# Weights times V as float32 products, both heads in turn on the two halves of TensorE's columns

## The chip, the core and the metric

The kernel runs on one core of a Trainium2 chip. In the profile its engines are PE (TensorE, the matmuls; PEld is its weight loads), DVE (VectorE), ACT (ScalarE), POOL (GpSimd) and SP (SyncE, which issues nearly all DMAs). The metric is the device time of one launch in microseconds, lower is better. Three runs of the kernel before gave 1402.59, 1403.88 and 1408.41 us.

## The reference

Attention with a band below the top score, and a gated feed-forward layer behind it, all in float32:

```
q, k, v: 8 batches x 8 heads x 576 x 64;  tau = 0.02
s    = q @ k.T / sqrt(64)                       per batch and head
keep = s >= max(s, row) - tau
a    = exp(s - max(s, row)) where keep, else 0
a    = a / (sum(a, row) + 1e-9)
x    = a @ v                                     -> 4608 tokens x 512
out  = (sigmoid(x @ w_gate) * (x @ w_val)) @ w_out   512 -> 1536 -> 512
```

## The kernel before, in words

A 576-token sequence is 4 tiles of 128 queries and 64 leftover queries. The attention works in visits, one for each batch (8) and pair of heads (4): 32 visits of 9 tiles: for each of the two heads (`h`) four query tiles, in groups of two, and one tile that holds the leftover queries of both heads (`h` is `None`, names with `_l`). The groups come in the order (`Visit.groups`): head 0 tiles 0 and 1, the leftover tile, head 0 tiles 2 and 3, head 1 tiles 0 and 1, head 1 tiles 2 and 3.

Most matmuls take their float32 operands as two float32r numbers each, a rounded high part and the remainder (low), and add three (or two) products; the first four visits (batch 0, `NPS` and `NPV`) do theirs as plain float32 matmuls, which stand in the profile as two records each. For a tile: the scores `s` (line 618, PE), the row maximum `st` (line 625, DVE), the threshold (line 630, ACT, or line 634, POOL), the exponential `p` (line 639, ACT), mask and row sum in one step (line 642, DVE). Then for a group: an addition to the sums (line 668, ACT, or 671, POOL), the reciprocal (line 674, DVE), and the scaling of `p` by POOL (line 687). PE transposes `p` into `tp` (line 702) and the leftover keys into `lk` (line 740, or 731 in the first four visits). In visits 4 to 31 the transposed weights are split: ACT copies the high part to `pt` (line 712), DVE subtracts for the low part (line 719), and the same for `pl` (lines 746 and 749); for a head's second group POOL copies the leftover queries' columns to the end of `pt` and `pl` (lines 759 and 762). V is loaded to `vn` and split into `vs` by ACT and POOL (lines 518 and 520). The product `av` (line 803) is nine matmuls a group and head, with V's high and low part side by side on the 128 columns of the stationary side; so the result's two halves of partitions are added, by a copy on ACT (line 806) and an addition on DVE (line 807), into `xf`. In the first four visits (line 790) the stationary side is V alone, 64 columns, so that one half of TensorE's columns is used; one copy on ACT (line 795) puts the result into `xf`.

The feed-forward layer works on blocks of 512 tokens. Blocks 0 to 4 go through `in_units` (`m`, line 861) and `out_units` (`o`, line 899), while attention runs on. The gate tile `th` is ACT's and then DVE's (lines 873 and 877). The last four blocks are taken two at a time (`two_blocks`) by Strassen's scheme: seven products p1 to p7 of sums of operands in place of eight (`qa`, `qb`, `qc`, line 1092; `ra`, `rb`, `rc`, line 1146); `token_sums` makes the operands (copies on ACT line 999, low parts on DVE line 1001, sums on POOL line 1006) and `chains` adds the results out of PSUM on DVE (lines 1029 and 1031). The weights come packed and are converted first, 36 tiles of them (`convert`: lines 425 to 469, with three steps on DVE, lines 441, 445 and 451, and two on POOL, lines 428 and 469).

The order of all instructions is written out before the program runs: `Plan.run` simulates the engines with the costs that each `op` carries, takes on each engine the ready operation with the smallest key for which buffers are free, and emits in that order. Keys count attention tiles: `LEAD` is how far ahead of its first tile a visit's loads are asked for, `SHIFT` a break in the keys ahead of batch 1, `CONV_IN` and `CONV_OUT` the first key and the step of the conversions, `SUMS` where the sums of weights for Strassen's scheme are spread. Feed-forward matmuls have keys above all attention, so they fill what attention leaves of PE. `SLOTS` is the number of buffers by tag; buffers of most tags are given in turn.

## Time and profile before

| | |
|---|---|
| median of three runs | 1403.88 us |
| the profiled execution: its time, its span | 1396.95 us, 1395.2 us |
| granted TensorE clock, mean | 0.999 |
| busy: PE, PEld | 1357.9, 1154.2 us |
| busy: DVE, ACT, POOL | 1097.0, 875.3, 801.4 us |
| DMA | 341.28 MB, mean 245 GB/s |
| first `m` to be gated on DVE (`th`) | 133.95 us |

In a row of groups stand: line, engine, operation, output<-inputs, shapes (partitions x elements), count; then busy time, mean ns of one; then the engine's idle time before them and what ended it. In a row of stretches: from:to, the length, and for each engine busy us and number of instructions, then the granted clock, the busy share of the DMA engines and GB/s. A row of waits names who waited, for whom, us in total, how often, and the longest. A row of the timeline begins with start and length in us. Matmuls overlap one another, so the distance from a start to the next one's start says more of PE than a length does.

### The profile page before, as it was taken

What the parts mean: (1) busy time and instruction counts of PE and PEld (TensorE: products, weight loads), DVE (VectorE), ACT (ScalarE), POOL (GpSimd) and SP (SyncE); (2) the same over time, 40 slices, a digit from 0 to 9 for tenths busy, and PEclk for the clock granted to TensorE, in tenths of its full rate; (3) what the DMA queues carried; (4) which work ended last, traced back from release to release, by engine and by line L of the source; (5) the groups of instructions that cost most, each with busy time, mean ns of one, the idle gap of its engine ahead of it and who ended that gap; (6) DMA issues with size and microseconds to landing.
All of it is one profiled execution on the core that took longest, in us unless ns stands there. A gap on an engine that the chain in (4) does not pass through costs nothing.

```text
span 1395.2 us, 23257 instructions
## 1 busy us (share of the span) xinstructions
PE 1357.9 (97%) x7472; PEld 1154.2 (83%) x7472; DVE 1097.0 (79%) x2144; ACT 875.3 (63%) x1930; POOL 801.4 (57%) x868
## 2 busy tenths in 40 slices
PE   7998999999999999999999999999999999899998
PEld 5666788888888888888888888888888887788886
DVE  7997989888788888888888888888936559645595
ACT  6877777677777777777777777777732235322242
POOL 5888765448787777786777976455420137001160
PEclk9999999999999999999999999999999999999999
DMA  7889888869999998899988999776567666665574
GB/s 266 279 248 314 303 260 238 230 205 264 267 261 330 292 278 250 261 289 296 304 267 242 303 295 277 200 224 198 160 223 227 201 195 202 202 199 187 184 225 137
DMA packets 142328, 341.28 MB, mean 245 GB/s; under 512 B 22784, under 2 KB 42752, under 8 KB 142208
## 3 DMA queue, kind: packets, MB, share of 16 engines
q1 hardware_dynamic: 142064, 339.80, 79.8%
q8 instruction: 61, 1.00, 0.3%
q14 instruction: 59, 0.48, 0.1%
q10 hardware_dynamic: 144, 0.00, 0.0%
HBM read 232.78 MB, written 55.57 MB: 207 GB/s over the span
## 4 chain that ended last, share of the span: by engine, by line
PE 78%; DMA 6%; DVE 6%; POOL 3%; ACT 2%; issue 2%; SPq 1%; DVEq 0%; ACTq 0%; POOLq 0%
PE m L861 17%; PE o L899 11%; PE s L618 9%; PE av L803 8%; PE qb L1092 7%; PE tp L702 6%; PE qa L1092 4%; PE qc L1092 4%; DMA su<-wid 4%; PE rb L1146 3%; PE av L790 2%; PE ra L1146 2%; PE rc L1146 2%; PE s_l L618 2%; POOL su L947 1%
## 5 line engine op out<-in xcount | busy, mean ns | idle before, releaser
L861 PE MATMUL m<-x,wi 128*128 128x512 f32 x1152 | 314.0, 403 | 0.0
L687 POOL TENSOR_SCALAR p<-p,w_t,sm 128x576 f32<-128x576 f32 x256 | 216.8, 857 | 91.5 <-DVE sm L674 80.7
L861 PEld LDWEIGHTS m<-x,wi 128*128 128x128 f32 x1152 | 200.9, 189 | 30.9
L642 DVE SCALAR_TENSOR_TENSOR p<-s,st,p 128x576 f32<-128x576 f32 x256 | 206.2, 812 | 23.0 <-ACT p L639 18.6
L625 DVE TENSOR_REDUCE st<-s 128x1 f32<-128x576 f32 x256 | 190.4, 751 | 34.1 <-PE s L618 30.1
L899 PE MATMUL o<-g,wo 128*128 128x512 f32 x720 | 194.3, 403 | 0.0
L639 ACT ACTIVATE p<-s,st 128x576 f32<-128x576 f32 x256 | 188.8, 738 | 6.9 <-DVE st L625 5.4
L712 ACT CAST pt<-tp 128x512 fp32r<-128x512 f32 x224 | 128.2, 587 | 63.5 <-PE tp L702 59.4
L719 DVE TENSOR_TENSOR pt<-tp,pt 128x512 fp32r<-128x512 f32 x224 | 150.5, 684 | 18.3 <-ACT pt L712 16.3
L618 PE MATMUL s<-kd,qd 128*128 128x288 f32 x896 | 159.7, 301 | 4.9 <-DVE p L642 2.7
L618 PEld LDWEIGHTS s<-kd,qd 128*128 128x128 f32 x896 | 136.8, 188 | 23.0 <-issue 3.0
L702 PE MATMUL tp<-ident,p 128*128 128x128 f32 x1024 | 146.8, 273 | 1.9 <-ACT pl_l L737 1.4
L899 PEld LDWEIGHTS o<-g,wo 128*128 128x128 f32 x720 | 126.1, 189 | 20.6 <-PE tp_l L702 0.2
L803 PE MATMUL av<-pt,vs 128*128 128x320 f32 (+1 forms) x896 | 137.0, 295 | 1.7 <-DVE pt L719 1.7
L702 PEld LDWEIGHTS tp<-ident,p 128*128 128x128 f32 x1024 | 122.3, 140 | 19.1 <-issue 3.2
L803 PEld LDWEIGHTS av<-pt,vs 128*128 128x128 f32 x896 | 129.2, 188 | 9.1 <-POOL p L687 2.1
L1006 POOL TENSOR_TENSOR gA<-gA 128x512 f32<-128x512 f32 x12 | 16.2, 1347 | 206.4 <-DVE gA L1071 206.4
L883 POOL TENSOR_TENSOR g<-th,g 128x512 fp32r<-128x512 f32 x60 | 78.8, 1313 | 23.0 <-ACT g L881 21.4
L806 ACT COPY avt<-av 64x256 f32<-64x256 f32 x112 | 44.2, 394 | 58.2 <-PE av L803 56.4
L1029 DVE TENSOR_TENSOR qu<-qb,qp 128x512 f32<-128x512 f32 x48 | 33.2, 691 | 55.9 <-PE qb L1092 48.4
L807 DVE TENSOR_TENSOR xf<-av,avt 64x256 f32<-64x256 f32 x112 | 50.8, 453 | 32.3 <-ACT avt L806 31.1
L749 DVE TENSOR_TENSOR pl<-lk,pl 64x128 fp32r<-64x128 f32 x224 | 64.7, 289 | 13.8 <-ACT pl L746 7.3
(171 smaller groups left out, 2743.1 us busy)
## 6 DMA issues: line engine op xcount, KB each, us to landing
wi<-wid SPq DMA_DIRECT2D x96, 512.0 KB, 7.1
kd<-k SPq DMA_DIRECT2D x112, 320.0 KB, 8.1
wo<-wod SPq DMA_DIRECT2D x60, 512.0 KB, 7.6
qd<-q SPq DMA_DIRECT2D x112, 128.0 KB, 6.1
wid<-ws SPq DMA_DIRECT2D x24, 512.0 KB, 4.5
su<-wid SPq DMA_DIRECT2D x24, 512.0 KB, 7.9
sid<-su SPq DMA_DIRECT2D x24, 512.0 KB, 4.6
wa<-wid SPq DMA_DIRECT2D x24, 512.0 KB, 4.5
```

The costliest lines, as they stand in the source:

```text
L618: nc.tensor.matmul(s.ap[:, c, :HALF], st(), mv(slice(k0 + c * HALF, k0 + (c + 1) * HALF)), start=m == 0, stop=m == len(steps) - 1,)
L625: op("DVE", 0.76, key, lambda: nc.vector.tensor_reduce(out=st.ap[:, 0:1], in_=sv(), axis=AX.XY, op=ALU.max, negate=True), reads=[s], write ...
L639: op("ACT", 0.74, key, lambda: nc.scalar.activation(p(), sv(), AF.Exp, bias=st.ap[:, 0:1], scale=1.0), reads=[s, (st, 0)], writes=[(g.p, i)])
L642: op("DVE", 0.9, key, lambda: nc.vector.scalar_tensor_tensor(out=p(), in0=sv(), scalar=st.ap[:, 1:2], in1=p(), op0=ALU.is_ge, op1=ALU.mult ...
L687: op("POOL", 0.9, key, lambda i=i: nc.gpsimd.tensor_scalar(out=p.ap[:, i * S : (i + 1) * S], in0=p.ap[:, i * S : (i + 1) * S], scalar1=w_t ...
L702: nc.tensor.matmul(tp.ap[:, c, :], self.p.ap[:, o + c * P : o + (c + 1) * P], ident, is_transpose=True, start=c == 0, stop=c == NJ - 1, sk ...
L712: op("ACT", 0.58, key, lambda: nc.scalar.copy(hi(), tp.ap), reads=[tp], writes=[(self.pt, (0, i))])
L719: op("DVE", 0.69, key, lambda: nc.vector.tensor_tensor(out=lo(), in0=tp.ap, in1=f32(hi()), op=ALU.subtract), reads=[tp, (self.pt, (0, i))] ...
L803: nc.tensor.matmul(av.ap, st, mv, start=i == 0, stop=i == len(ms) - 1)
L861: nc.tensor.matmul(m.ap, wv[:, a, c * P : (c + 1) * P], xs[c].ap[:, z, c0:c1], start=e == 0, stop=e == 11,)
L899: nc.tensor.matmul(acc.ap, wv[:, f, a], g[fg * ND + f].ap[:, z], start=(fg, f, a, z) == (0, 0, 0, 0), stop=(fg, f, a, z) == (NFG - 1, ND - ...
L1092: nc.tensor.matmul(acc.ap, wv[:, y, (2 * h + c) * P : (2 * h + c + 1) * P], xt[prod][c].get()[:, z], start=e == 0 and prod in FIRST, stop= ...
```

## The change

The split of the transposed weights and of V goes, in all visits. V is loaded as it is, with six column groups per head in place of five: the leftover keys' rows come twice, once with zeros in the second half of the partitions and once with zeros in the first half, so that the transposed leftover keys of two tiles (one `lk` of 128x128) can be used with all 128 rows. `pt` and `pl` hold both heads of a pair of tiles (`of_tiles`), and the product of both heads is one operation, issued after head 1's group: for each chunk of keys one float32 matmul of head 0 with its output on partitions 0 to 63 and one of head 1 on partitions 64 to 127, in turn. The leftover queries are multiplied from the leftover tile's own `pt` by matmuls of 64 columns. One copy by ACT puts both heads' result into `xf`. The addition to the sums goes; a factor on q that is zero where tau is negative, and a maximum on tau, take its place. POOL's scaling stays a tensor_scalar with two operations, whose first now adds a tile of zeros.

With it go: one more `t2` buffer and two tags moved in `chains`; other constants for the plan (`LEAD`, `CONV_IN`, `SHIFT`, `SUMS`); three of the output weights' conversions end on DVE instead of POOL (`DVE_LO_OUT`); `token_sums` puts some of POOL's subtractions on DVE (`X_BY`, `G_BY`) and one of them earlier; and `out_two` does, for every product but p1, all matmuls of one half of the outputs (`e`) ahead of the other's.

```diff
-    "w": 7, "t2": 5,
+    "w": 7, "t2": 6,
-LEAD = 8
-CONV_IN, CONV_OUT = (8, 2.2), (24, 3)
+LEAD = 3
+CONV_IN, CONV_OUT = (12, 2.2), (24, 3)
-NPS, NPV = 4, 4
+NPS = 4
+AV_COST = 0.0093
-SHIFT = 30
+SHIFT = 20
-DVE_LO_IN, DVE_LO_OUT = (), ()
+DVE_LO_IN, DVE_LO_OUT = (), range(6, 12, 2)
-SUMS = (36, 4)
+SUMS = (36, 6)
+X_BY = ((("POOL",) * 4, ("DVE",)), (("DVE",) * 4, ("DVE",)))
+G_BY = (("POOL", "DVE", "POOL", "DVE"), ("DVE",))
...
+            self.vs = buf("vs", [P, NJ + 2, 2, D], F32, f"vs{n}")
+            op("SP", 1.2, key - 3, lambda: nc.sync.dma_start(out=self.vs.ap, in_=v[b, hp]), writes=[self.vs])
...
         def normalise(self, key):
             sm, p, n = self.sm, self.p, self.n
-            if DEN(self.vis.first) == "ACT":
-                op("ACT", 0.3, key, lambda: nc.scalar.activation(sm.ap[:, :n], sm.ap[:, :n], AF.Identity, bias=den_t[:, 0:1]),
-                   writes=[sm])
...
             op("PE", 0.44, key, go, reads=[(self.p, i)], writes=[tp], also=[self.pt])
-            op("ACT", 0.58, key, lambda: nc.scalar.copy(hi(), tp.ap), reads=[tp], writes=[(self.pt, (0, i))])
...
-                op("DVE", 0.69, key, lambda: nc.vector.tensor_tensor(
-                    out=lo(), in0=tp.ap, in1=f32(hi()), op=ALU.subtract
-                ), reads=[tp, (self.pt, (0, i))], writes=[(self.pt, (1, i))])
+            op("ACT", 0.58, key, lambda: nc.scalar.copy(self.pt.ap[:, self.z, :, i * P : (i + 1) * P], tp.ap),
+               reads=[tp], writes=[(self.pt, (self.z, i))])
...
+        def output(self, c, key):
+            vis, pt, pl = self.vis, self.pt, self.pl
+            last = self.tiles[0] != 0
+            W = 2 * P + (SL if last else 0)
+            av = buf("b", [P, W], F32, f"av{self.name}", "att")
+            c0 = self.tiles[0] * P
+            ms = [(0, 2 * P, j, lambda h, j=j: pt.ap[:, h, j]) for j in range(NJ)]
+            ms += [(i * P, (i + 1) * P, NJ + i, lambda h: pl.ap[:, h]) for i in range(2)]
+            if last:
+                sl = lambda h: slice(h * SL, (h + 1) * SL)
+                ms += [(2 * P, W, j, lambda h, j=j: c.pt.ap[:, 0, j, sl(h)]) for j in range(NJ)]
+                ms += [(2 * P, W, NJ + 1, lambda h: c.pl.ap[:, 0, sl(h)])]
+            def go():
+                for i, (a, z, j, m) in enumerate(ms):
+                    for h in range(2):
                         nc.tensor.matmul(
+                            av.ap[h * D : (h + 1) * D, a:z], vis.vs.ap[:, j, h], m(h),
+                            start=i == 0, stop=i == len(ms) - 1, skip_group_check=True,
                         )
+            op("PE", AV_COST * W, key, go,
+               reads=[pt, pl] + ([c.pt, c.pl] if last else []) + [vis.vs], writes=[av], also=[vis.xf])
+            last_att[0] = op("ACT", act(W), key, lambda: nc.scalar.copy(vis.xf.ap[:, c0 : c0 + W], av.ap),
+                             reads=[av], writes=[(vis.xf, self.name)])
...
-                for e in range(2):
+                ws.append(w)
+            for g, e in [(g, e) for g in range(NFG) for e in range(2)] if prod == "p1" else [(g, e) for e in range(2) for g in range(NFG)]:
```

The plan's order moves in three places. The first is PE in visit 4 (batch 1, names `_0_`), while block 0's `m` runs: `av` is a product, `pt` and `pl` its transposed weights, `vs` V. Before, head 0's first pair of tiles:

```order
L861 MATMUL m_3_0_0_1807<-x_0_593,ws_0_619 128x512 x2
L803 MATMUL av_0_00_1816<-pt_0_00_1686,vs_0_1193 128x256 x8
L803 MATMUL av_0_00_1816<-pl_0_00_1754,vs_0_1193 128x256
L861 MATMUL m_3_0_0_1807<-x_0_593,ws_0_619 128x512
L861 MATMUL m_3_0_0_1807<-x_1_909,ws_0_619 128x512
```

and in the change, both heads' first pair, ahead of it the last transpose of leftover keys that it needs (`lk`):

```order
L673 MATMUL lk_0_10_1824<-ident,p_0_10_1661 128x128
L757 MATMUL m_4_1_0_1799<-x_2_1143,ws_1_970 128x512
L757 MATMUL m_4_1_0_1799<-x_3_1388,ws_1_970 128x512 x3
L757 MATMUL m_5_0_0_1834<-x_0_565,ws_0_1494 128x512 x3
L757 MATMUL m_5_0_0_1834<-x_1_848,ws_0_1494 128x512 x3
L595 MATMUL s_1_001_1849<-kd_1_0_1446,qd_1_0_1465 128x288 x4
L697 MATMUL av_0_10_1855<-pt_0_00_1614,vs_0_1135 64x256 x8
L697 MATMUL av_0_10_1855<-pl_0_00_1632,vs_0_1135 64x128 x4
L595 MATMUL s_1_l_1883<-k_1_1407,q_1_1444 128x288 x6
```

Further on, on PE still, the same visit's second pair, with the leftover queries of both heads (`pt_0_l`, `pl_0_l`):

```order
L757 MATMUL m_6_0_0_1969<-x_1_848,wi_6_0a 128x512
L697 MATMUL av_0_12_1994<-pt_0_02_1723,vs_0_1135 64x256 x8
L697 MATMUL av_0_12_1994<-pl_0_02_1768,vs_0_1135 64x128 x4
L697 MATMUL av_0_12_1994<-pt_0_l_1540,vs_0_1135 64x64 x8
L697 MATMUL av_0_12_1994<-pl_0_l_1556,vs_0_1135 64x64 x2
L659 MATMUL tp_1_000_2036<-ident,p_1_00_1819 128x128 x4
```

The product of one head moved behind the other head's tiles, and three operand shapes (256, 128 and 64 columns) stand where one stood.

The second is DVE ahead of the first gate tile `th`; `wb` and `wa` are weights being converted, three rows each. Before:

```order
L545 SCALAR_TENSOR_TENSOR q_1_1522<-qn_1_1438,q_1_1522 128x640
L441 TENSOR_SCALAR wb_1_1539<-wa_1_1512 128x512
L445 SCALAR_TENSOR_TENSOR wb_1_1539<-wr_1_1449,wb_1_1539 128x512
L451 SCALAR_TENSOR_TENSOR wa_1_1512<-wr_1_1449,wb_1_1539 128x512
L441 TENSOR_SCALAR wb_0_1559<-wa_0_1537 128x512
L445 SCALAR_TENSOR_TENSOR wb_0_1559<-wr_0_1467,wb_0_1559 128x512
L451 SCALAR_TENSOR_TENSOR wa_0_1537<-wr_0_1467,wb_0_1559 128x512
L642 SCALAR_TENSOR_TENSOR p_0_00_1530,sm_0_00_1584<-s_0_000_1498,st_0_000_1520,p_0_00_1530 128x576
L642 SCALAR_TENSOR_TENSOR p_0_00_1530,sm_0_00_1584<-s_0_001_1515,st_0_001_1524,p_0_00_1530 128x576
L877 SCALAR_TENSOR_TENSOR th_0_0_1572<-th_0_0_1572,m_0_1_0_1568 128x512
```

and in the change:

```order
L602 TENSOR_REDUCE st_0_000_1418<-s_0_000_1402 128x1
L428 TENSOR_SCALAR wb_1_1430<-wa_1_1396 128x512
L432 SCALAR_TENSOR_TENSOR wb_1_1430<-wr_1_1332,wb_1_1430 128x512
L438 SCALAR_TENSOR_TENSOR wa_1_1396<-wr_1_1332,wb_1_1430 128x512
L619 SCALAR_TENSOR_TENSOR p_0_00_1435,sm_0_00_1457<-s_0_000_1402,st_0_000_1418,p_0_00_1435 128x576
L602 TENSOR_REDUCE st_0_001_1467<-s_0_001_1420 128x1
L646 RECIPROCAL sm_0_l_1412<-sm_0_l_1412 128x1
L602 TENSOR_REDUCE st_0_020_1480<-s_0_020_1469 128x1
L522 SCALAR_TENSOR_TENSOR q_1_1444<-qn_1_1365,scale_t,q_1_1444 128x640
L773 SCALAR_TENSOR_TENSOR th_0_0_1453<-th_0_0_1453,m_0_1_0_1449 128x512
```

Counted over DVE's whole order, 27 conversions are complete ahead of this `th` before, and 23 in the change; the other nine and thirteen come after it.

The third is PE in the last stretch, the second pair of blocks: `rb_0` and `rb_1` are the banks of the two halves of the outputs, and p7 and then p4 go to both. Before, the place where p7 ends and p4 begins:

```order
L1146 MATMUL rb_0_16047<-gs_p_1_16097,wo_p_1_16079 128x512 x6
L1146 MATMUL rb_0_16047<-gs_p_q_16118,wo_p_2_16099 128x512 x3
L1146 MATMUL rb_0_16047<-gs_p_ptc,wo_p_2_16099 128x512 x3
L1146 MATMUL rb_0_16047<-gs_p_0_16140,wo_p_0_16120 128x512 x3
L1146 MATMUL rb_0_16047<-gs_p_1_16144,wo_p_0_16120 128x512 x3
L1146 MATMUL rb_0_16047<-gs_p_2_16160,wo_p_1_16142 128x512 x3
L1146 MATMUL rb_0_16047<-gs_p_3_16164,wo_p_1_16142 128x512 x3
L1146 MATMUL rb_0_16047<-gs_p_4_16177,wo_p_2_16162 128x512 x3
L1146 MATMUL rb_0_16047<-gs_p_5_16181,wo_p_2_16162 128x512 x3
L1146 MATMUL rb_1_16062<-gs_p_0_16077,wo_p_0_16056 128x512 x6
L1146 MATMUL rb_1_16062<-gs_p_1_16097,wo_p_1_16079 128x512 x6
```

and in the change:

```order
L1049 MATMUL rb_0_14478<-gs_p_q_14647,wo_p_2_14582 128x512 x3
L1049 MATMUL rb_0_14478<-gs_p_ptc,wo_p_2_14582 128x512 x3
L1049 MATMUL rb_1_14494<-gs_p_0_14503,wo_p_0_14534 128x512 x6
L1049 MATMUL rb_1_14494<-gs_p_1_14536,wo_p_1_14561 128x512 x6
L1049 MATMUL rb_1_14494<-gs_p_q_14647,wo_p_2_14582 128x512 x3
L1049 MATMUL rb_1_14494<-gs_p_ptc,wo_p_2_14582 128x512 x3
L1049 MATMUL rb_0_14478<-gs_p_0_14611,wo_p_0_14624 128x512 x3
L1049 MATMUL rb_0_14478<-gs_p_1_14613,wo_p_0_14624 128x512 x3
L1049 MATMUL rb_0_14478<-gs_p_2_14622,wo_p_1_14627 128x512 x3
L1049 MATMUL rb_0_14478<-gs_p_3_14629,wo_p_1_14627 128x512 x3
L1049 MATMUL rb_0_14478<-gs_p_4_14672,wo_p_2_14649 128x512 x3
L1049 MATMUL rb_0_14478<-gs_p_5_14677,wo_p_2_14649 128x512 x3
```

In both, bank `rb_0` is finished ahead of `rb_1`; in the change `rb_1`'s p7 stands between `rb_0`'s p7 and `rb_0`'s p4.

More of the change, by code (lines that the diff above doesn't have):

```diff
@@ L1 @@
 import heapq
+import itertools
 from contextlib import ExitStack
@@ L991, in __init__, with token_sums @@
             self.b, self.get, self.part = b, get, part
-    def token_sums(base, dst, key):
+    def token_sums(base, dst, key, sums_by, lows_by):
         b11, b12, b21, b22 = base
+        engine = {"DVE": nc.vector, "POOL": nc.gpsimd}
+        lows = itertools.cycle(lows_by)
         def put(src, to):
```

224 lines of the change are left out of this document (54 added, 170 removed).

## Prediction

> **What bounds the kernel now.** I read the engine table first, then busy time by stretches, then who waited for whom on the engine that bounds. The rows: the span, the busy time of each engine, and three stretches, cut after the first gate tiles and where attention ends.
>
> ```profile
> span 1395.2 us, 23257 instructions
> PE 1357.9 (97%) x7472; PEld 1154.2 (83%) x7472; DVE 1097.0 (79%) x2144; ACT 875.3 (63%) x1930; POOL 801.4 (57%) x868
> core 0: us, PE busy (x) PEld busy (x) DVE busy (x) ACT busy (x) POOL busy (x), PEclk, DMA share, GB/s
> 0.00:142.30 142.30, 125.48 (x666) 88.76 (x666) 118.71 (x242) 108.40 (x211) 111.23 (x156) 0.99 0.83 279
> 142.30:1030.00 887.70, 879.55 (x5262) 776.59 (x5263) 751.39 (x1610) 658.03 (x1534) 599.75 (x653) 1.00 0.87 257
> 1030.00:1395.00 365.00, 352.91 (x1546) 288.86 (x1544) 226.91 (x293) 108.88 (x187) 90.44 (x60) 1.00 0.62 201
> ```
>
> PE is the bound from about 140 us on: 879.55 of 887.70 us in the middle stretch, 352.91 of 365.00 in the last. So relief of DVE, ACT or POOL is worth there only what PE still waits for, and a dearer matmul is paid in full. The start is different: PE has 16.8 us free and DVE is as full. What ends the start is the first `th`, which DVE can do only when its queue of softmax steps and weight conversions has come that far:
>
> ```profile
> L441 DVE TENSOR_SCALAR wb<-wa 128x512 int32<-128x512 int32 x28 | 19.2, 685 | 1.1 <-POOL wa L428 1.1
> L445 DVE SCALAR_TENSOR_TENSOR wb<-wr,wb 128x512 int32<-128x512 int32 x27 | 18.7, 692 | 0.5
> L451 DVE SCALAR_TENSOR_TENSOR wa<-wr,wb 128x512 int32<-128x512 int32 x27 | 18.4, 682 | 0.4
> DVE st L625 <- PE s L618: 8.8, 15, 1.7
> 133.95 0.68 DVE L877 SCALAR_TENSOR_TENSOR th<-th,m 128x512 f32<-128x512 f32 x1
> ```
>
> (DVE's groups and waits up to 142.3 us, and its timeline.) One conversion costs DVE 0.685 + 0.692 + 0.682 = 2.06 us; in all that stretch DVE waited 8.8 us for PE's scores.
>
> **Part 1, the product itself: +14 us.** Two pieces of PE's timeline, columns start and length. The first is the old product in the middle stretch, a pair of tiles of one head without and with the leftover queries; the second is the form with float32 products that the first four visits already use, one head at a time.
>
> ```profile
> 402.54 1.12 PE L803 MATMUL av<-pt,vs 128*128 128x256 f32 x8
> 403.50 0.28 PE L803 MATMUL av<-pl,vs 128*128 128x256 f32 x1
> 403.62 0.27 PE L740 MATMUL lk<-ident,p 128*128 128x128 f32 x1
> ...
> 408.36 1.33 PE L803 MATMUL av<-pt,vs 128*128 128x320 f32 x8
> 409.53 0.31 PE L803 MATMUL av<-pl,vs 128*128 128x320 f32 x1
> 409.68 0.27 PE L740 MATMUL lk<-ident,p 128*128 128x128 f32 x1
> ```
>
> ```profile
> 61.52 1.94 PE L790 MATMUL av<-pt,vp 128*64 128x256 f32 x8
> 63.39 0.64 PE L790 MATMUL av<-pl,vp 64*64 64x256 f32 x2
> 63.96 1.09 PE L702 MATMUL tp<-ident,p 128*128 128x128 f32 x8
> ...
> 67.14 1.94 PE L790 MATMUL av<-pt,vp 128*64 128x256 f32 x8
> 68.92 0.63 PE L790 MATMUL av<-pt_l,vp 128*64 128x64 f32 x8
> 69.48 0.64 PE L790 MATMUL av<-pl,vp 64*64 64x256 f32 x2
> 69.96 0.27 PE L790 MATMUL av<-pl_l,vp 64*64 64x64 f32 x2
> 70.17 0.66 PE L702 MATMUL tp<-ident,p 128*128 128x128 f32 x4
> ```
>
> From start to the next instruction's start, the old form takes 1.08 and 1.32 us, so 4.80 us for the four products of a visit. The float32 form takes 2.44 and 3.03 us for one head, 10.94 for a visit. A float32 matmul stands as two records. The new code streams the same columns (four times 256 and twice 128 in place of five times 256) but all with 128 rows; the two records with 64 rows cost 0.57 against 0.47 at the pace of the eight before them (1.87 / 8 = 0.234 each), and so about 0.1 in each of the four products falls away: 10.5 us one after another. Both heads at once on the two halves halve that, if the halves overlap: 5.3 us.
>
> No row shows two halves at once. Bounds: at the best pace of the rows (8 records in 1.78 us, 8 of 64 columns in 0.56) 32 records of 256, 16 of 128 and 20 of 64 come to 10.3, halved 5.15. If records start in order, the second head trails the first by one record, 0.234 in each of two products: 5.74. Without overlap 10.5. I take 5.3, as the row-built middle: 28 visits x (5.3 - 4.80) = +14 us (10 to 26 with overlap). The first four visits get cheaper for PE by 5.6 us each, but there DVE ends the stretch, so this is counted at nothing; if DVE weren't there, it would be worth 22 us.
>
> The Trainium skill (TensorEngine Tiling (Array Packing), Key Properties) says that different tiles can execute weight loads and matmuls in parallel and that a change of tiling mode drains the array. The first half is the whole of this term and no run here shows it yet; the second agrees with the 64-row records above, 0.285 each against 0.234.
>
> **Part 2, what DVE, ACT and POOL lose.**
>
> ```profile
> L719 DVE TENSOR_TENSOR pt<-tp,pt 128x512 fp32r<-128x512 f32 x224 | 150.5, 684 | 18.3 <-ACT pt L712 16.3
> L749 DVE TENSOR_TENSOR pl<-lk,pl 64x128 fp32r<-64x128 f32 x224 | 64.7, 289 | 13.8 <-ACT pl L746 7.3
> L520 POOL TENSOR_TENSOR vs<-vn,vs 128x640 fp32r<-128x640 f32 x28 | 44.1, 1574 | 33.6 <-ACT vs L518 33.6
> ```
>
> The two subtractions alone are 215 us of DVE, and POOL's split of V goes; ACT loses its copies of V and its additions to the sums. What of it PE waited for in the middle:
>
> ```profile
> PE s L618 <- DVE p L642: 1.9, 4, 0.8
> PE av L803 <- DVE pt L719: 1.7, 1, 1.7
> PE m L861 <- DVE th L877: 1.1, 1, 1.1
> PE s_l L618 <- DVE p L642: 0.8, 1, 0.8
> PE m L861 <- ACT th L873: 0.7, 1, 0.7
> PE s L618 <- DVE p_l L642: 0.7, 2, 0.5
> ```
>
> That is 6.9 us between 150 and 1030 us, all behind DVE or ACT. I count -6 (0 to -7). The change adds a wait: a product now needs both heads' transposed weights, and the next visit's transposes wait for one of the two `pt` buffers that it frees. In the planned order other matmuls stand between the last of these transposes and the product, enough to hide a copy; I count nothing, and where that cover is gone PE stands for one copy, as in the 1.7 us row.
>
> **Part 3, the start: -11 us.** In DVE's order 27 conversions stood before the first `th`, now 23: 4 x 2.06 = -8.2 us, and one subtraction of 128x512 moves from POOL to DVE there, at L719's 684 ns: -7.5. The four moved conversions fall into the stretch that has just lost 215 us of DVE work, which covers them; without that cover they would cost their 8 us again. PE's lighter first visits shorten DVE's 8.8 us of waiting for scores; I take -3.5 of it. Together -11 (-4 to -16). Loads are asked for five tiles later (`LEAD`); three buffers of `kd` and `qd` cover that. V's load grows from five column groups to six, on DMA engines with 0.87 of their time taken, and comes a visit ahead into two buffers: nothing, unless it lands late.
>
> **Part 4, the end: -6 us.** PE's waits after 1030 us:
>
> ```profile
> PE rb L1146 <- issue: 2.5, 2, 1.7
> PE rc L1146 <- DMA wo_p<-sod: 1.8, 2, 1.1
> PE qb L1092 <- DVE qu L1029: 1.4, 1, 1.4
> PE rb L1146 <- ACT gs_p L999: 1.3, 1, 1.3
> PE rb L1146 <- DVE gs_p_ptc L1001: 0.7, 1, 0.7
> PE rb L1146 <- DVE gs_p_q L1001: 0.6, 1, 0.6
> ```
>
> 8.3 us. Product p4 waits on the bank that DVE still reads for p7 (`rb`); with all of one half's matmuls before the other's, DVE has 18 matmuls' time for it. Half of the subtractions move from POOL to DVE, which is busy 227 of 365 us there. I count -6 (0 to -8).
>
> Sum: +14 - 6 - 11 - 6 = -9 us on the profiled execution's 1396.95 us (its span and 1.75 around it), that is 1388. The median of the runs shown, 1403.88, lies 6.9 above it, so 1395 us.
>
> **The rivals.** *No overlap.* PE takes the two halves one after the other: 28 x (10.5 - 4.80) = +160, less 23, 1541 us. For it: every float32 record in the trace follows the last at full length. Against it: those were always of one half. Chance 0.07.
>
> *Overlap, and still dearer (the other side).* The second head trails (5.74), and the 20 records of 64 columns, 0.07 us each, are held by their weight loads, twice as many in the same time, and gain nothing by overlap: +0.7, 6.4 us a visit, +46 - 23 = +23, 1427 us. It decides from 5.62 us a visit, where 28 x 0.82 eats the 23. Chance 0.15. The Trainium skill (TensorE: Matmul & The Clock Gate, Measured speedup vs the span model) gives 2.38 times for three column tiles, an efficiency of 0.79; as an estimate by that page 10.5 / 1.59 = 6.6 us, +50, 1431 us.
>
> *Nothing measurable.* The trailing record is paid in full, +26, or the start is held by POOL's and ACT's share of the conversions instead of DVE's: -23 + 26 gives 1407, the forecast without the start 1406. For it: POOL 111 and ACT 108 of 142 us. Chance 0.23.
>
> *Clearly faster.* Halves at 5.15 (+10), all 8.8 us of DVE's waits gone (-16), and all of PE's waits (-15): 1383 us. Chance 0.2.
>
> **How the numbers follow.** The forecast, 1395 give or take 7, has 0.35. A measurement here can't tell 0.5% (7 us) from no change. Faster by more: 0.2 and four fifths of 0.35, 0.48. Slower by more: 0.15 + 0.07, with 0.01 from the third case, 0.23. Between: 0.29. Range 1378 to 1428: it holds the forecast, the third case and most of the second and fourth, and leaves out the first; the forecast's own is 1388 to 1402.
>
> **What would show it.** A product without leftover queries should take 2.4 to 2.6 us on PE, and records of the two halves should lie over one another; 4.7 would mean no overlap. The first `th` should start near 123 us instead of 133.95. PE's waits behind DVE between 150 and 1030 us should be near 1 us, and `rb` should not wait for issue. I am wrong if a visit's products cost over 5.7 us, or if the first `th` is not earlier.

## The result, and the profile after

| | before | after |
|---|---|---|
| median of four runs | 1403.24 us | 1416.89 us |
| ratio | 1 | 1.0103, 95% interval 1.0068 to 1.0138 |
| profiled execution: time, span | 1396.95, 1395.2 us | 1413.75, 1411.5 us |
| granted TensorE clock, mean | 0.999 | 0.991 |
| first gate tile (`th`) starts | 133.95 us | 126.39 us |

The change makes the kernel slower by 1.0%. The forecast was 1395 us, faster; the time lies in its range, and its sign is wrong. The traces are of single executions, which lie 6 us (before) and 3 us (after) under these medians, so sums over a trace hold for that execution.

The page of the kernel after (the span and the busy times), and its stretches, cut as those of before:

```profile
span 1411.5 us, 23674 instructions
PE 1359.0 (96%) x8384; PEld 1117.6 (79%) x8384; DVE 836.3 (59%) x1560; ACT 763.1 (54%) x1576; POOL 650.7 (46%) x683
```

```profile
0.00:142.30 142.30, 113.55 (x720) 85.04 (x720) 120.28 (x240) 102.48 (x192) 103.43 (x141) 0.96 0.81 270
142.30:1030.00 887.70, 870.80 (x6019) 723.83 (x6018) 493.97 (x994) 548.85 (x1193) 505.22 (x513) 0.99 0.85 258
1030.00:1411.00 381.00, 374.63 (x1649) 308.78 (x1647) 222.01 (x328) 111.76 (x191) 42.09 (x31) 1.00 0.63 201
```

DVE lost 257 us of work in the middle stretch, as the change says. PE is nevertheless busy for 870.80 of 887.70 us there, against 879.55 before: it stands 8.8 us longer. The clock's column reads 0.99 and not 1.00. The first `th` and one pair of products, from DVE's and PE's timelines:

```profile
126.39 0.68 DVE L773 SCALAR_TENSOR_TENSOR th<-th,m 128x512 f32<-128x512 f32 x1
```

```profile
250.27 1.10 PE L757 MATMUL m<-x,wi_1a 128*128 128x512 f32 x4
251.29 1.95 PE L697 MATMUL av<-pt,vs 128*64 128x256 f32 x16
253.07 0.61 PE L697 MATMUL av<-pl,vs 128*64 128x128 f32 x8
253.61 0.66 PE L659 MATMUL tp<-ident,p 128*128 128x128 f32 x4
```

From 251.29 to 253.61 the product of both heads takes 2.32 us, where one head alone took 2.44 in the first visits of the kernel before: the halves run at once. Over the 28 visits behind the first `th` the distances from start to start come to 147.9 us, 5.28 a visit. Two stops that follow straight on a product, at 412.33 and 878.40 us, stand in that sum with 2.1 us; without them it is 5.21 a visit. The last matmul ahead of a product, though, is followed 320 to 325 ns after its start (median) in place of 228. That is some 0.09 us for each of the 56 products, 5.3 us, which stand in no row of `av`.

What PE waited for in the middle (140 to 1030 us) and behind 1050 us:

```profile
PE tp L659 <- POOL p L648: 6.2, 7, 1.7
PE s L595 <- DVE p L619: 4.0, 4, 2.4
PE s_l L595 <- DVE p L619: 2.6, 1, 2.6
PE m L757 <- DMA wi_0a<-wid: 1.8, 1, 1.8
```

```profile
PE rb L1049 <- DVE gs_p L900: 1.9, 2, 1.3
PE rc L1049 <- DVE gs_p L900: 1.2, 1, 1.2
```

The largest item of the middle, `tp` behind POOL's scaling of `p`, stands at nothing in the kernel before. At the end the wait of `rb` for issue has gone. Some of the stops seem to cost twice, as these stretches of the kernel after show (the clock is the third column from the right):

```profile
216.00:219.60 3.60, 0.97 (x6) 0.74 (x7) 3.37 (x7) 2.71 (x6) 3.60 (x5) 1.00 0.35 146
219.60:229.80 10.20, 7.04 (x24) 5.46 (x23) 8.40 (x15) 5.36 (x11) 10.20 (x10) 0.50 0.81 274
724.80:728.20 3.40, 3.33 (x13) 3.04 (x14) 1.54 (x3) 1.38 (x4) 1.62 (x2) 0.50 1.06 318
```

PE works for 0.97 of 3.60 us, and then has half the clock for 10.2 us. At 724.8 us the same follows a stop of 2.4 us. The kernel before has no such window between 140 and 1030 us. The lengths, 3.4 and three times 3.4 us, agree with the Trainium skill (TensorE: Matmul & The Clock Gate, What's actually happening), which says that the gate counts activity in windows of 3413 ns.

From the first `th` to the start of the last matmul, all of PE's starts sorted by what lies between them (us; a stop is a distance of over 0.3 us more than the pace):

| | before | after | difference |
|---|---|---|---|
| products, start to start | 134.3 | 147.9 | +13.6 |
| extra in the record ahead of a product | 0.0 | 5.3 | +5.3 |
| stops while attention runs | 9.6 | 13.6 | +4.0 |
| excess in windows at half clock | 0.0 | 8.4 | +8.4 |
| stops behind attention | 10.0 | 4.2 | -5.8 |
| all other work | 1103.2 | 1101.6 | -1.6 |
| sum | 1257.1 | 1281.0 | +23.9 |

With the first `th` 7.6 us earlier that is +16.3 us, the difference of the spans. The row of half clock holds two stops inside the first window as well, 1.38 and 1.78 us of idle PE.

Where do the stops come from? The first window stands among conversions of weights. Nine of their steps take DVE between 209.77 and 218.47 us; here are the last of them and the mask `p` behind it (DVE), and what PE waits for (PE):

```profile
217.78 0.69 DVE L438 SCALAR_TENSOR_TENSOR wa<-wr,wb 128x512 int32<-128x512 int32 x1
218.39 0.81 DVE L619 SCALAR_TENSOR_TENSOR p<-s,st,p 128x576 f32<-128x576 f32 x1
```

```profile
219.26 1.55 PE L595 MATMUL s_l<-k,q 128*128 128x288 f32 x6 [2.63 <-DVE p L619]
222.19 1.97 PE L659 MATMUL tp<-ident,p 128*128 128x128 f32 x8 [1.38 <-POOL p L648]
226.15 4.25 PE L757 MATMUL m<-x,wi_0a 128*128 128x512 f32 x10 [1.78 <-DMA wi_0a<-wid]
```

At 222.19 us POOL's scaling of `p` comes straight behind its own steps of the conversion, and at 226.15 us `m` waits for a weight that was converted just before. The second window follows one long step on DVE (DVE, then PE):

```profile
719.46 4.54 DVE L522 SCALAR_TENSOR_TENSOR q<-qn,scale_t,q 128x640 fp32r<-128x640 f32 x1
724.88 1.30 PE L595 MATMUL s<-kd,qd 128*128 128x288 f32 x4 [2.40 <-DVE p L619]
```

The median of these 28 steps is 1.13 us. POOL ran without a pause from 709.33 to 723.31 us meanwhile; why the step took so long was not tried. Split at 300 us, stops while attention runs and half clock together went from 3.5 to some 11.7 us ahead of it, and from 6.1 to some 10.4 us behind it.

### The profile page after: what moved, and what is told of

Its sections match the earlier page's. It is cut to its first block, busy times and chain, and to the rows that moved or that the text cites. A ratio compares the mean times of both kernels' runs of the same rounds, so it can differ in the third digit from the quotient of the medians.

```text
span 1411.5 us, 23674 instructions
## 1 busy us (share of the span) xinstructions
PE 1359.0 (96%) x8384; PEld 1117.6 (79%) x8384; DVE 836.3 (59%) x1560; ACT 763.1 (54%) x1576; POOL 650.7 (46%) x683
## 4 chain that ended last, share of the span: by engine, by line
PE 70%; DMA 12%; DVE 7%; POOL 5%; issue 2%; SPq 2%; ACT 2%; ACTq 0%; POOLq 0%; DVEq 0%
PE m L757 15%; PE o L795 11%; PE av L697 7%; PE s L595 7%; PE qb L991 7%; PE tp L659 5%; PE qa L991 5%; PE qc L991 4%; DMA kd<-k 3%; PE rb L1049 3%; DMA su<-wid 2%; PE ra L1049 2%; PE rc L1049 1%; DMA wo<-wod 1%; DVE p L619 1%
## 5 line engine op out<-in xcount | busy, mean ns | idle before, releaser
L648 POOL TENSOR_SCALAR p<-p,zero_t,sm 128x576 f32<-128x576 f32 x256 | 208.6, 823 | 190.5 <-DVE sm L646 156.0
L757 PE MATMUL m<-x,wi 128*128 128x512 f32 x1152 | 293.9, 397 | 0.0
L795 PE MATMUL o<-g,wo 128*128 128x512 f32 x720 | 186.4, 399 | 0.4 <-DMA wo<-wod 0.4
L665 ACT COPY pt<-tp 128x512 f32<-128x512 f32 x256 | 147.3, 588 | 54.4 <-PE tp L659 52.0
L595 PEld LDWEIGHTS s<-kd,qd 128*128 128x128 f32 x896 | 134.0, 191 | 20.0 <-issue 6.4
L697 PE MATMUL av<-pt,vs 128*64 128x256 f32 x1024 | 127.3, 389 | 0.7 <-ACT pt L665 0.4
L773 DVE SCALAR_TENSOR_TENSOR th<-th,m 128x512 f32<-128x512 f32 x60 | 41.2, 686 | 125.0 <-PE m L757 79.7
L697 PEld LDWEIGHTS av<-pt,vs 128*64 128x64 f32 x1024 | 68.9, 138 | 51.1 <-issue 11.1
L607 ACT ACTIVATE st<-st,ntau_t 128x1 f32<-128x1 f32 x224 | 67.0, 299 | 53.4 <-DVE st L602 52.8
L991 PE MATMUL qa<-xs_p,wa 128*128 128x512 f32 x288 | 73.1, 389 | 0.0
L843 POOL TENSOR_TENSOR su<-su 128x256 f32<-128x256 f32 (+1 forms) x60 | 60.5, 1010 | 25.0 <-DMA su<-wid 20.1
```

The lines of the kernel that those rows point to most:

```text
L595: nc.tensor.matmul(s.ap[:, c, :HALF], st(), mv(slice(k0 + c * HALF, k0 + (c + 1) * HALF)), start=m == 0, stop=m == len(steps) - 1,)
L648: op("POOL", 0.9, key, lambda i=i: nc.gpsimd.tensor_scalar(out=p.ap[:, i * S : (i + 1) * S], in0=p.ap[:, i * S : (i + 1) * S], scalar1=zer ...
L665: op("ACT", 0.58, key, lambda: nc.scalar.copy(self.pt.ap[:, self.z, :, i * P : (i + 1) * P], tp.ap), reads=[tp], writes=[(self.pt, (self.z ...
L697: nc.tensor.matmul(av.ap[h * D : (h + 1) * D, a:z], vis.vs.ap[:, j, h], m(h), start=i == 0, stop=i == len(ms) - 1, skip_group_check=True,)
L757: nc.tensor.matmul(m.ap, wv[:, a, c * P : (c + 1) * P], xs[c].ap[:, z, c0:c1], start=e == 0, stop=e == 11,)
L795: nc.tensor.matmul(acc.ap, wv[:, f, a], g[fg * ND + f].ap[:, z], start=(fg, f, a, z) == (0, 0, 0, 0), stop=(fg, f, a, z) == (NFG - 1, ND - ...
```

## The experiments

All kernels compute all of the reference's steps. `tail_only`, `no_product`, `split_slack` and `no_product_sums` keep the split product, `product_only` and `product_only_sums` the end of before; the others hold the instructions of the kernel after in another order. The first four take the change apart: the product, the constants of the start (`LEAD`, `CONV_IN`; `SHIFT` alone moves no instruction), and the end (`out_two`, `token_sums`, `DVE_LO_OUT`, `t2` and `chains`, `SUMS`). "Gaps" are PE's stops of over 0.3 us between 140 and 1030 us, windows at half clock included; "half clock" is the length of these windows there; "sums" are POOL's waits there that the profile puts down to loads of `su` and `so`, the operands of the sums of weights for Strassen's scheme.

| kernel | us | ratio to before (95%) | first `th` | gaps | half clock | sums |
|---|---|---|---|---|---|---|
| before | 1403.24 | 1 | 134.0 | 10.1 | 0 | 19.3 |
| after | 1416.89 | 1.0103 (1.0068 to 1.0138) | 126.4 | 20.7 | 13.7 | 34.3 |
| consts | 1418.06 | 1.0102 (1.0076 to 1.0129) | 132.6 | 19.9 | 6.8 | 68.5 |
| tail_only | 1406.24 | 1.0028 (1.0011 to 1.0046) | 134.5 | 17.1 | 3.4 | 19.7 |
| no_product | 1398.10 | 0.9969 (0.9953 to 0.9985) | 132.9 | 9.7 | 3.4 | 12.7 |
| product_only | 1430.70 | 1.0205 (1.0182 to 1.0229) | 131.4 | 22.7 | 13.7 | 44.6 |
| paced | 1438.02 | 1.0251 (1.0218 to 1.0284) | 134.2 | 30.2 | 20.5 | 33.0 |
| late_sums | 1430.15 | 1.0192 (1.0162 to 1.0221) | 128.2 | 11.3 | 10.2 | 10.1 |
| slack | 1416.54 | 1.0089 (1.0059 to 1.0119) | 146.8 | 10.0 | 6.8 | 35.6 |
| one_after_other | 1532.42 | 1.0924 (1.0884 to 1.0965) | 138.3 | 7.2 | 6.8 | 6.8 |
| slack_mid | 1406.81 | 1.0016 (1.0000 to 1.0032) | 128.1 | 14.1 | 6.8 | 31.7 |
| in_sums_late | 1403.73 | 0.9988 (0.9970 to 1.0005) | 129.8 | 10.7 | 10.2 | 16.7 |
| slack_and_sums | 1402.09 | 0.9982 (0.9964 to 1.0000) | 128.9 | 15.0 | 3.4 | 25.5 |
| split_slack | 1410.72 | 1.0039 (1.0015 to 1.0063) | 138.0 | 23.8 | 6.8 | 36.2 |
| nudge | 1420.03 | 1.0128 (1.0096 to 1.0160) | 133.2 | 19.5 | 6.8 | 47.0 |
| product_only_sums | 1415.63 | 1.0096 (1.0060 to 1.0133) | 131.9 | 17.3 | 6.8 | 16.5 |
| no_product_sums | 1402.73 | 0.9997 (0.9976 to 1.0018) | 135.2 | 10.3 | 3.4 | 4.6 |

Each ratio is against runs of the kernel before on the same chip; these had medians from 1401.89 to 1404.51 us, so differences of two medians of the table hold to some 3 us.

### The change in its parts

`product_only`, the kernel before with the product alone; and `consts`, the kernel after with the constants of the start put back:

```diff
 # consts, against the kernel after; product_only has these two lines and the end of before
-LEAD = 3
-CONV_IN, CONV_OUT = (12, 2.2), (24, 3)
+LEAD = 8
+CONV_IN, CONV_OUT = (8, 2.2), (24, 3)
...
 # consts alone
-SHIFT = 20
+SHIFT = 30
```

> The kernel before with the product alone (float32, both heads in turn, no splits, and the factor on q that goes with it); the constants LEAD and CONV_IN, the order of out_two and token_sums are those of before. Theory A (plan): +15 us for the products, -6 us of PE's waits behind DVE in the middle, -5 us at the start (24 to 25 conversions ahead of the first gate tile in place of 27): 1403 + 4 = about 1407 us. Theory B (product): +15, and +10 us of new waits, and half-clock windows that follow them: 1422 us or more.

> The kernel after with two constants of the plan as they were before: LEAD 8 instead of 3 (loads asked for eight tiles ahead) and CONV_IN (8, 2.2) instead of (12, 2.2) (conversions earlier). Product, end and all else as in the kernel after. Theory A (plan): the product costs about the +15 us it was costed at, and the 22 us that were not foreseen (16.6 us of new PE waits of over 0.3 us between 140 and 1030 us, and 17 us of windows at half the granted clock, 8.5 us lost) come from constants that leave tiles and converted weights just in time. Then this kernel gives back some 4 us of the start (24 conversions ahead of the first gate tile instead of 23, and loads that compete earlier), and the waits and the half-clock windows in the middle go: 1416.9 - 18 = about 1398 us. Theory B (product): the waits come from the product itself, which needs both heads' transposed weights before it can start and frees its pt buffer late, so the constants change nothing there: 1417 to 1421 us, with PE's gaps in the middle still near 20 us.

`tail_only`, the kernel before with the end alone, and `no_product`, which adds the constants of the start:

```diff
 # no_product, against the kernel before; tail_only has only the end
-LEAD = 8
-CONV_IN, CONV_OUT = (8, 2.2), (24, 3)
+LEAD = 3
+CONV_IN, CONV_OUT = (12, 2.2), (24, 3)
-DVE_LO_IN, DVE_LO_OUT = (), ()
+DVE_LO_IN, DVE_LO_OUT = (), range(6, 12, 2)
-SUMS = (36, 4)
+SUMS = (36, 6)
...
-            token_sums([base[c, 0], base[c, 1], base[c + 2, 0], base[c + 2, 1]], {p: xt[p][c] for p in SEVEN}, key)
+            token_sums([base[c, 0], base[c, 1], base[c + 2, 0], base[c + 2, 1]], {p: xt[p][c] for p in SEVEN}, key,
+                       *X_BY[k])
```

> The kernel before with only the end of the change: the order of out_two, the subtractions of token_sums that move to DVE (X_BY, G_BY), three output weights' conversions that end on DVE, t2 of 6, SUMS (36, 6). The product stays split, the constants of the start stay. Both theories: the end gives what the prediction said, -6 us, as PE's gaps after attention fell from 9.97 to 3.65 us in the kernel after: 1397 us (-4 to -8). If the end's gain isn't real (PE only does the same work later), 1403 us.

> All of the change but the product: as the kernel tail_only, and with LEAD 3 and CONV_IN (12, 2.2). Theory A (plan): the constants hurt the split product too, as loads are asked for five tiles later and conversions come later: PE's gaps in the middle rise by 8 us or more over the 10.1 us of the kernel before, so 1403 us or more, and half-clock windows appear near 220 us. Theory B (product): the constants by themselves help (26 conversions ahead of the first gate tile, -2 to -4 us): 1393 to 1396 us, gaps in the middle as before.

The constants did not bring the loss: putting them back leaves the time where it was, and without the product they go with the fastest kernel of all, 0.9969 of before. The loss is with the product: alone it costs 2.0%, and on top of `no_product` it costs 19 us (1416.89 against 1398.10). Theory A fell in the form in which it was put. The parts don't add up: the end, which costs the split product 4 us, takes some 14 us off the kernel with the new one (1.0205 in `product_only`, 1.0102 in `consts`).

The end alone did not give its 6 us. The gap it was meant to close closed, but another opened, at 1052 us, PE's and then POOL's row of waits between 1040 and 1070 us in `tail_only`:

```profile
PE qb L1099 <- ACT xs_p L1005: 6.2, 1, 6.2
```

```profile
POOL xb L1013 <- DMA xb<-xp: 11.8, 1, 11.8
```

The gaps in the middle rose too, from 10.1 to 17.1 us. At 1052 us POOL stands before a load of the first operands of Strassen's scheme, ACT behind POOL, PE behind ACT. In the kernel after, where attention ends about 100 us earlier (its last product starts at 920 us in place of 1024), this does not happen.

### Is it the overlap?

```diff
-                for i, (a, z, j, m) in enumerate(ms):
-                    for h in range(2):
+                for h in range(2):
+                    for i, (a, z, j, m) in enumerate(ms):
```

> The kernel after with the loops of the product exchanged: all of head 0's matmuls ahead of head 1's, in place of in turn; all else as in the kernel after. If records of the two halves truly run at once only when they alternate, the products of a visit cost 10.5 us in place of 5.4: 28 x 5.1 = +143 us behind the start, and some 5 to 20 us more in the first four visits where PE has little free: 1565 to 1580 us. If the halves did not overlap, or if the order of issue did not matter, 1417 us.

PE's timeline, the first and the last row of one product without leftover queries and what follows it:

```profile
273.06 1.94 PE L697 MATMUL av<-pt,vs 128*64 128x256 f32 x8
...
276.63 0.60 PE L697 MATMUL av<-pl,vs 128*64 128x128 f32 x4
277.16 0.66 PE L659 MATMUL tp<-ident,p 128*128 128x128 f32 x4
```

4.10 us in place of 2.32, and 9.53 a visit in place of 5.28. The order of issue decides whether the halves run at once, and the overlap is worth 115 us of this kernel's time. One after the other was cheaper than the 10.5 us I had worked out, so the time came out below the expected 1565.

### Is it lost pacing?

```diff
 # paced: line 619, the cost of the mask in the plan
-        op("DVE", 0.9, key, lambda: nc.vector.scalar_tensor_tensor(
+        op("DVE", 1.8, key, lambda: nc.vector.scalar_tensor_tensor(
```

> The kernel after with one planning cost changed: the mask step on DVE (line 619) is planned with 1.8 us instead of 0.9 us. What is computed, and every instruction, stay; only the order moves: in the plan attention is paced by DVE again, as it was by the subtractions that the change removed, and 2042 of the 2160 matmuls of blocks 0 to 4 stand ahead of the last product (2102 in the kernel before, 1544 in the kernel after). Theory P (lost pacing): with DVE relieved, attention's tiles run just in time for PE, so every lateness stops PE, and the granted clock halves behind a stop. Then PE's gaps of over 0.3 us between 140 and 1030 us fall from 20.7 to about 10, and the half-clock windows go: 1417 - 17 = 1400 us. Theory Q (POOL's queue): PE waits because POOL, in order, waits for the loads of the sums of weights (34 us in the kernel after, 19 before) ahead of scaling p; pacing spreads the loads, and gives 5 us at most: 1412. Theory R (the product itself): the waits are of the product's own path, both heads' transposed weights and the change of tile mode; pacing gives nothing: 1417 us.

Attention ended at 1056 us, paced as meant, but the gaps rose to 30.2 us, most of them between 198 and 247 us: the higher planned cost also put off conversions, and one wait of `s` alone took 6.8 us. Theory P's figure of 1400 us is far off. The edit moved two things, so it does not rule pacing out behind 250 us; it gave no sign for it either.

### Is it POOL's queue?

POOL and PE in the kernel after, two places of the timeline, and the waits of POOL between 140 and 1030 us, after and then before:

```profile
432.53 1.24 SPq L839 DMA_DIRECT2D su<-wid  x1
...
434.94 1.28 POOL L843 TENSOR_TENSOR su<-su 128x512 f32<-128x512 f32 x1 [3.34 <-DMA su<-wid]
436.20 1.63 POOL L648 TENSOR_SCALAR p<-p,zero_t,sm 128x576 f32<-128x576 f32 x2
...
437.08 0.66 PE L659 MATMUL tp<-ident,p 128*128 128x128 f32 x4 [1.43 <-POOL p L648]
```

```profile
873.27 2.91 POOL L843 TENSOR_TENSOR so<-so 128x512 f32<-128x512 f32 x3 [4.14 <-DMA so<-wod]
876.14 0.73 POOL L843 TENSOR_TENSOR so<-so,so 128x256 f32<-128x256 f32 x1
876.82 0.72 POOL L843 TENSOR_TENSOR so<-so 128x256 f32<-128x256 f32 x1
877.53 1.62 POOL L648 TENSOR_SCALAR p<-p,zero_t,sm 128x576 f32<-128x576 f32 x2
...
878.40 0.66 PE L659 MATMUL tp<-ident,p 128*128 128x128 f32 x4 [1.73 <-POOL p L648]
```

```profile
POOL su L843 <- DMA su<-wid: 20.1, 12, 3.3
POOL so L843 <- DMA so<-wod: 14.2, 3, 9.3
```

```profile
POOL su L947 <- DMA su<-wid: 12.6, 8, 3.4
POOL so L947 <- DMA so<-wod: 6.7, 5, 2.1
```

In these places POOL comes to an addition for Strassen's weights, stands for the load, adds, and only then scales the `p` that PE's transpose is waiting for. In the kernel before such a wait reached PE too, by way of ACT and DVE (POOL, ACT, DVE, PE):

```profile
355.79 1.28 POOL L947 TENSOR_TENSOR su<-su 128x512 f32<-128x512 f32 x1 [3.36 <-DMA su<-wid]
361.86 1.14 ACT L958 CAST su<-su 128x512 fp32r<-128x512 f32 x2 [2.59 <-POOL su L947]
363.51 0.69 DVE L719 TENSOR_TENSOR pt<-tp,pt 128x512 fp32r<-128x512 f32 x1 [2.88 <-ACT pt L712]
364.35 1.41 PE L803 MATMUL av<-pt,vs 128*128 128x320 f32 x8 [1.68 <-DVE pt L719]
```

The loads are not later than before. Each kernel's row of DMA issues, after and before, ends with the median time from issue to landing:

```profile
su<-wid SPq DMA_DIRECT2D x24, 512.0 KB, 7.5
```

```profile
su<-wid SPq DMA_DIRECT2D x24, 512.0 KB, 7.9
```

POOL has less to do ahead of them: relieved of V's split and the leftover copies, it has 505 us of work in the middle stretch in place of 600. That it comes to the loads sooner for that reason is argued. The plan counts 4.1 us for such a load where no other is ahead of it (1.7 for the transfer, 2.4 ahead of and behind it), the chip takes 7.5. In `late_sums` the first additions of each sum are planned 10 us behind their loads:

```diff
...
-            add(1.3, lambda t=t: full(t, 0), lambda t=t: full(t, 0), lambda t=t: full(t, 1), 1, [], [t])
+            add(1.3, lambda t=t: full(t, 0), lambda t=t: full(t, 0), lambda t=t: full(t, 1), 1, [], [t], lag=10.0)
```

> The kernel after with one planning number added: POOL's first additions of each sum of weights (line 843) are planned 10 us after their loads have landed in the plan, so that POOL doesn't stand in front of a load that is late on the chip. What is computed stays. Theory Q (POOL's queue): POOL's waits for the loads of sums fall from 34 us to under 5, and PE's waits behind POOL's p with them: -10 us, 1407 us. Theory P (lost pacing) and theory R (the product itself): POOL's waits fall, PE's gaps stay near 20 us: 1415 to 1417 us.

In the middle it did what theory Q said: gaps of 11.3 us. But the last sums of output weights came so late that their use at the end waited, PE's longest wait between 1170 and 1210 us:

```profile
PE rc L1049 <- DMA wo_p<-sod: 17.5, 1, 17.5
```

So `in_sums_late` does it for the sums of input weights alone:

```diff
...
-            add(1.3, lambda t=t: full(t, 0), lambda t=t: full(t, 0), lambda t=t: full(t, 1), 1, [], [t])
+            add(1.3, lambda t=t: full(t, 0), lambda t=t: full(t, 0), lambda t=t: full(t, 1), 1, [], [t], lag=0.0 if name[0] == "o" else 10.0)
```

> The kernel after with POOL's first additions planned 10 us behind their loads for the sums of input weights alone (the first twelve), not for those of output weights, which in the kernel late_sums came so late that PE stood 17.5 us for a load of them at 1188 us. What is computed stays. Theory Q (POOL's queue): in the kernel late_sums PE's gaps between 140 and 1030 us fell from 20.7 to 11.3 us, and its waits behind POOL's p from 6.2 to 0.9, so this kernel keeps that and loses the stop at the end: 1417 - 9 = 1408 us. If POOL's queue does not matter, 1417 us.

1403.73 us, 13 us less than the kernel after, at no measurable distance from before. Its rows of the same waits, and its middle stretch:

```profile
PE tp L659 <- POOL p L648: 0.3, 1, 0.3
POOL so L843 <- DMA so<-wod: 16.7, 4, 7.4
```

```profile
142.30:1030.00 887.70, 879.16 (x6070) 731.52 (x6069) 496.56 (x1003) 550.71 (x1202) 513.84 (x518) 0.99 0.86 258
```

PE is busy 879.16 us there, as before the change (879.55).

Any edit of the plan gives another order, so three more runs ask whether another order alone would have done it: a control that leaves the sums alone, and the same edit where POOL waited most, and where it waited little.

```diff
 # nudge
-AV_COST = 0.0093
+AV_COST = 0.0097
```

> A control: the kernel after with the planned cost of a product raised by 4% (AV_COST 0.0097 in place of 0.0093), which touches neither the sums nor the slack, but gives another order (25 conversions ahead of the first gate tile, 1528 of 2160 feed-forward matmuls ahead of the last product). Theory Q (POOL's queue): POOL still waits some 30 us for the loads of sums in the middle, and the time stays with the kernel after, 1412 to 1420 us. Theory L (luck of the order): any other order is likely to be better than that of the kernel after, and the 13 us of the kernel in_sums_late say nothing of the sums; then this one may come to 1400 to 1408 us too, with POOL's waits for sums unchanged.

> The kernel product_only (1430.7 us; there POOL waited 44.6 us for the loads of sums) with the additions for the sums of input weights planned 10 us behind their loads. Theory Q (POOL's queue): those waits fall by half or more, PE's gaps between 140 and 1030 us from 22.7 to about 12, and the time by 12 us to about 1418; what is left over the kernel before is the product's 19 us (14 in the products, 5 in the record ahead of each), less the start. Theory L (luck of the order): any time between 1415 and 1432, with gaps that don't follow POOL's waits.

> The kernel no_product (split product, 1398.1 us; there POOL waited 12.7 us for the loads of sums, and PE never behind them for more than 1.3 us) with the same edit of the sums. Theory Q (POOL's queue): next to nothing to gain, 1396 to 1399 us; the kernel in_sums_late stands 5 to 8 us over it, which is the price of the product without its stops. Theory L (luck of the order): 1390 to 1410 us, with gaps that don't follow POOL's waits.

The control stayed at 1420 us, with 47.0 us of POOL's waits. `product_only` fell by 15 us, from 1430.7 to 1415.6. The split product gained nothing (1402.7 against 1398.1), and `in_sums_late` stands 1 us over it, where 5 to 8 were expected. So the edit of the sums takes 13 and 15 us off the two kernels with the new product, and other orders that leave the sums alone (`nudge`, `consts`) did not. The gain lies behind 300 us: stops and half clock while attention runs, added up as in the table of the result, fall there from some 10.4 to 0.9 us, and from 16.5 to 1.7 us on `product_only` (`nudge` 9.8, `consts` 15.1). Ahead of 300 us they don't fall: 11.7 and 12.5 us, 11.0 and 15.1 us.

How the edit does it is shown only in part. Followed back through what each waited for, PE's stops of over 0.25 us between 140 and 1030 us lead to POOL at a load of `su` or `so` for 4.5 of 16.6 us in the kernel after, 3.8 of 16.8 in `product_only`, 7.9 of 14.8 in `consts`, 2.7 of 14.5 in the control, and for none in `in_sums_late` and `product_only_sums`. But it is 4.5 of 7.9 us in the kernel before as well. And POOL's waits don't set the time: `consts` has twice those of the kernel after and the same time, and `slack_mid`, below, is 10 us faster with nearly the same. In `product_only` the longest stop, 2.91 us, stands behind ACT, which itself stood 4.92 us for a load. That the other stops behind 300 us follow from POOL's queue is not shown.

### Does more slack in the plan help?

```diff
 # slack
-LAG = {"PE": 1.2, "DVE": 0.3, "ACT": 0.2, "POOL": 0.08, "SP": 0.08}
+LAG = {"PE": 2.4, "DVE": 0.3, "ACT": 0.2, "POOL": 0.08, "SP": 0.08}
 # slack_mid, split_slack, slack_and_sums
-                        lag = 0.0 if s.eng == x.eng else LAG[s.eng]
+                        lag = 0.0 if s.eng == x.eng else LAG[s.eng] + (1.2 if s.eng == "PE" and now > 140 else 0)
```

> The kernel after with the plan's lag ahead of an instruction of PE 2.4 us instead of 1.2: whatever PE takes from another engine is planned to be ready 1.2 us earlier, so that PE has other matmuls ahead of it. What is computed stays. Theory P (lost pacing) and theory Q (POOL's queue): most of PE's stops are shorter than 1.2 us or are shortened by it, gaps in the middle fall by half, -10 us, though the first gate tile comes later (28 conversions ahead of it in place of 23, +8 to +10 us): about 1417 us, with gaps near 10. Theory R (the product itself): gaps stay near 20 us, and the start is lost: 1425 us.

> The kernel after with the plan's lag ahead of an instruction of PE 2.4 us instead of 1.2, but only behind 140 us of the plan's own time, so that the start stays as in the kernel after (23 conversions ahead of the first gate tile). What is computed stays. Theory S (thin slack): the product costs PE 16 us (11 in the products' pace, 5 in the record ahead of each), and the rest of the loss are stops of PE, and the clock windows behind them, because the plan lets PE come to an operand just as it is planned to be ready. In the kernel slack the stretch behind the first gate tile took 1265.6 us against 1281.0 in the kernel after; with the start kept, that is 1417 - 15 = 1402 us. Theory R (the product itself): the gain in the kernel slack was only work moved ahead of the first gate tile, and this kernel takes 1414 to 1417 us.

> Both edits at once: the lag of 2.4 us for PE behind 140 us of the plan's time, and the additions for the sums of input weights 10 us behind their loads. Theory S (thin slack): the two take away the same stops in part: 1398 to 1402 us, PE's gaps between 140 and 1030 us under 8 us. Theory R (the product itself): 1412 to 1417 us.

> The kernel no_product (split product as before, all else of the change) with the lag of 2.4 us for PE behind 140 us of the plan's time. It is the pair of the kernel slack_mid: the two differ by the product and what goes with it alone, with the same slack. Theory S (thin slack): the kernel no_product had 9.7 us of gaps in the middle, of which 3 may go: 1395 us; slack_mid stands 4 to 10 us over it, since of the product's 16 us the earlier start (6.5 us) is to be taken off. Theory R (the product itself): 1395 us too, and slack_mid 18 us or more over it.

`slack` halved the gaps of the middle (20.7 to 10.0 us) and lost the gain at the start, 20 us where I expected 8 to 10. With the start kept, `slack_mid` took 10 us off the kernel after, and both edits together 15; that isn't the sum of 10 and 13, so they take away the same stops in part. The gaps stayed at 15.0 us with both, where under 8 were expected. On the split product the same slack cost 10 to 13 us (1.0039 against 0.9969, 1410.7 against 1398.1 us; gaps of 23.8 us). Slack is thus no remedy by itself, and theory S, which expected 1395 us there, is wrong on this pair: a later order of PE also frees buffers later, which the kernel with the full DVE can't afford; that this is the reason is argued, not shown.

## Why the prediction was wrong

**Part 1, the product, +14: right, and one item short.** 5.28 us a visit against the 5.3 taken, +13.6 us (+11.9 without the stops that stand in those rows); no leaning on the trailing bound (5.74). The rivals "no overlap" and "overlap, and still dearer" by 5.62 us did not come about: with the record ahead a visit costs 5.28 + 5.3 / 28 = 5.47. That item, 5.3 us, stands where the tiles change, which I had seen only inside the old 64-row records and had not charged at the 56 products' entry; no run separates the change of tiles from anything else there. The Trainium skill (TensorEngine Tiling (Array Packing), Key Properties) lists a drain on a change of mode; I quoted it and put no number on it.

**Part 2, PE's waits in the middle, -6: this is the step that failed.** Of the rows behind DVE and ACT that I wanted to strike, those on `pt` and `th` went (3.5 us), but those on `p` rose from 3.4 to 6.6 us, where I had named 1 us as the mark. I counted what DVE's relief takes away, and not what the new order brings. The plan moved attention forward (its last product from 1024 to 920 us) and conversions back. Stops in the middle came to +4.0 us and the windows at half clock, with the stops inside them, to +8.4: +12.4 us where -6 was predicted, a miss of 18 us. Some 8 us of it arose ahead of 300 us, at the conversions; POOL's first addition for a sum starts only at 355.3 us there, so its waits at loads have no part in this. Behind 300 us some 4 us arose, as much as the stop behind DVE's step of 4.54 us and its window cost. The waits on `p` that I wanted to strike are these: 2.63 us behind conversions, 2.40 us behind that step. POOL's waits at loads, which my experiments went after, reach PE for 4.5 us in both kernels, though the edit of the sums takes away nearly all stops behind 300 us. The half-clock windows were in no term: the row of before read 1.00, and I took it for fixed. "I count nothing" for the product's wait for both heads held: PE's `av` waited 0.4 us in all for ACT's copies.

**Part 3, the start, -11: right in kind, 7.6 us.** The first `th` came at 126.39 instead of 123. The cover for the four moved conversions, the stretch that DVE's relief was to leave free, did not hold: the stops and the window around 220 us stand at conversions. That moving them made these stops is not shown: with the conversions of before, `product_only` has 11.0 us of stops and half clock ahead of 300 us, and `no_product`, with the moved ones and the split product, has 7.4, the kernel before 3.5.

**Part 4, the end, -6: right, -5.8 us,** in the kernel after. `tail_only` shows that it isn't a property of the edit alone: there the same edit cost 4 us: a load came in its way, and the gaps of the middle rose by 7 us.

**The sum.** 13.6 + 5.3 + 12.4 - 7.6 - 5.8 - 1.6 (all other work) = +16.3 us against -9. Two rivals lie equally near by their number, "nothing measurable" (1407) and "overlap, and still dearer" (1427, with the right sign); the reason of neither came about, so that is luck. That the time fell into the range is luck too. No rival had new stops of PE in the middle in it. POOL's rows of waits in the kernel before showed 19.3 us at these loads, and the 1.7 us of `av` that I put down to DVE goes back to one of them.

What stays open, besides what brings the stops, is the product's price without them. `in_sums_late` and `no_product_sums` stand at 0.9988 and 0.9997, and `no_product` at 0.9969; the intervals overlap. So these runs leave the float32 product within some 0.4% of the split one, either way. By its median the fastest kernel that was run is the change without its product.

## What to carry to other kernels

When a change relieves engines that don't bound, it also gives a new order: work comes sooner, and may stand behind other work or at a load, although nothing was added. Follow each long stop back to where it starts before you name a cause, in the kernel before too: a wait booked on DVE began at POOL there, and the queue that seemed the culprit after had cost as much before. Compare the planned time of a load with the one measured (4 against 7.5 us here) before trusting an order. And read the clock column stretch by stretch: behind a stop of PE of 2.4 us the window at half clock cost another 1.7 us.
